# New priorities and new landing times for the planner of a fused attention and mixture-of-experts kernel

## Chip, cores and metric

The kernel runs on one core of one Trainium2 chip. The metric is device time in microseconds (us) of one execution. A core has four compute engines that the text names as the profile does: PE (TensorE, matmuls), DVE (VectorE), ACT (ScalarE) and POOL (GpSimd). SP (SyncE) mostly issues DMAs. Each engine takes its own instructions strictly in the order in which the program gave them to it.

## What is computed

Sliding-window attention with four sink tokens, and behind it a mixture of eight experts, of which each token takes the best two:

```python
scores = scale * np.matmul(q, k.transpose(0, 1, 3, 2))      # q, k, v: 4 x 8 x 768 x 64
keep = is_sink | in_window                                  # 4 sinks, window 128
scores = np.where(keep, scores, -1000000000.0)
scores = scores - np.max(scores, axis=-1, keepdims=True)
a = np.exp(scores)
a = a / (np.sum(a, axis=-1, keepdims=True) + 1e-09)
x = np.matmul(a, v)                                         # to 3072 tokens x 512
...
logits = x @ w_gate
noise_scale = np.log1p(np.exp(x @ w_noise))
noisy_logits = logits + noise_scale * noise
top2 = np.argpartition(-noisy_logits, 2, axis=1)[:, :2]     # weights: softmax over the two
...
h = np.maximum(x[mask] @ w1[e], 0.0)                        # 512 -> 1024, per expert
out[mask] += top2_w[mask, k, None] * (h @ w2[e])            # 1024 -> 512
```

## The kernel before

**Staging.** Part one (`phase_one`) is attention, the routing of the first three batches, and what the first expert needs. Part two (`phase_two`) is the routing of the last batch and the eight experts. Attention goes over 16 head pairs `g`, each in three tiles `n` of 2 x 128 queries, 48 tiles in all. Each tile is a chain over all engines. PE computes scores into a PSUM bank `S` (`qk`, L401). ACT copies the block before the diagonal (`prev`, L405) and DVE the diagonal block under its mask (`cur`, L410 and L412) into `cbuf`. DVE takes the row maximum (`mins`, L422), POOL subtracts it (`sub`, the helper of line 305), ACT takes the exponential (`exps`, L429), and DVE sums it for two tiles at once (`sums`, L432). PE turns the result (`ptr`, L464), ACT copies it to `CT` (`ptr_c`, L467), and DVE or POOL mask it to `CM` (`ptr_m`). The sinks go a way of their own: ACT copies them (`pcopy`, L451), PE turns them (L459), ACT copies them to `ps` (`sink_c`, L493) and PE multiplies (`sinks`, L502). PE multiplies with the values `vn` (L486) and with the difference of neighbouring value blocks `dv` (L489; the difference itself is line 305 on DVE or POOL). ACT copies the sum to `turned` (`pv_c`, L511), PE turns it back (`rows`, L516), DVE or ACT scale it (`rows_c`, L525), and SP stores it to `x_rows` in memory (L532).

Beside it run the logits of a batch (L710 to L726), its routing (L789 and on: the two best experts, a rank within each expert from a mask `m` by matmuls at L824, lists of tokens, L856 to L882), the gathers of the first expert's rows (`sg`, `xg`, issued by POOL), and the turning of these rows for PE (`rows_turn`, PE at L1093, ACT at L1102, DVE at line 305).

**Weights.** All weights are split into a rounded part and a remainder. For each chunk of 512 KB, `w_chunk` lets SP load it to a buffer `st` (L1129), ACT round it into `wr` or `w2a` (`hi`, L1138), and DVE or POOL take the remainder (`lo`). Five chunks of the first expert are loaded in part one. The same two `st` buffers hold the sinks' values, which ACT rounds to `vr` (L357). The first expert's matmuls are L1066 to L1068 (up) and L1337 to L1339 (down); a ReLU on ACT (L1318) and its remainder on DVE (L1326) lie between.

**What sets the order.** No order is written by hand. Every step is recorded by `Plan.op` with its engine, an assumed duration and a priority. `Plan.run` then plans: the engine that is free first takes, of its steps whose inputs are there by its reckoning, the one with the lowest number. The steps are emitted by planned start, and this is the order of each engine's queue. A transfer is planned as an SP step and a "DMA" step of assumed length `us`, and is taken to land a little later: 1.2 us, 0.6 more for a long one, plus `late`.

```python
    def dma(self, prio, fn, us, r=(), w=(), u=(), n=1, late=0):
        ...
        self.op("SP", .48 * n, prio, fn, r, list(w) + [("dma", d)], u, lat=.65)
        self.op("DMA", us, prio, None, list(r) + [("dma", d)], w, u, lat=1.2 + (.6 if us > .7 else 0) + late)
```

In attention a step's priority is its tile number plus a fraction plus `P(g, name)`: the table `PR` has one number for each kind of step, with an extra for the first two and last two head pairs, and the table `BY` has one more for each kind and each of the 16 pairs. Other steps of part one have numbers in `PR`: `ga` gathers, `gt` turning of gathered rows, `lg` logits, `rt` routing of the first three batches, `w1` the first expert's weights. Part two has its own table `P2`; its plan starts from the state in which the plan of part one ends. At run time the engines wait for semaphores, whatever the plan assumed.

Of the kernel before, what the change touches and what calls it, by code (L numbers as in the profile page):

```python
# [30 lines left out]
BY = dict(cur=(0, -1.82, -0.09, -4.77, 35.24, 11.33, 2.04, -10.64, 0.52, 0, -1.01, -3.26, 14.21, 1.62, 0.09, -1.4),
          cur1=(0.93, -1.05, -2.09, 0, -2.58, -1.8, -0.49, -4.53, 1.67, 0.36, -1.49, 1.77, 5.16, 0, 49.28, -0.04),
          mins=(6.57, 0.21, 57.07, 0.23, 0, -0.65, -13.4, 4.24, 13.09, -2.13, 0, -0.06, -0.69, 2.29, 67.31, 0.72),
          sub=(-1.09, 44.64, -1.41, -0.42, 4.26, 1.23, -3.67, -0.5, -0.79, 1.56, 235.35, 0.77, -1.93, -0.06, 2.36, 0),
          exps=(-7.52, 7.26, 2.07, 0.74, 0.15, -1.72, -0.45, -37.83, 0.43, 53.75, 1.62, -265.24, 1.55, -22.19, -1.22,
          2.06), sums=(0.42, -1.37, 9.97, 6.54, 0, 1.48, 1.11, 4.08, -5.15, -0.49, 0, 15.68, -4.9, -0.05, 7.41, 0),
          sums_i=(-0.24, 4.03, 0, -2.92, -0.07, -47.94, -0.24, 0.08, -0.02, 267.66, 10.52, 3.51, -12.76, 1.73, -1.63,
          0.51), pcopy=(-133.07, -3.49, 0.13, 0.44, -5.06, 2.59, -0.29, -3.31, 1.66, -3.27, -1.06, 2.44, -3.33, -1.68,
          231.11, -0.12), plow=(0, 0, 6.4, 0.11, 3.22, -9.99, 0, -0.73, 0, 0, 23.53, 0.11, -6.2, 1.96, 8.99, -409.97),
          ptr=(2.11, -1.38, -12.28, -2.62, 0.43, -21.26, -0.4, -5.17, 246.76, -0.54, -2.13, 38.22, -1.99, -1.89, 6.88,  # L40
          -1.57), ptr_c=(1.99, 16.57, -4.61, 1.02, -0.92, 0.3, 54.42, -6.52, 0, 0, 0, 35.55, -0.02, 0.04, -2.65,
          0.51), ptr_m=(41.67, 0, 2.33, -3.62, 18.7, -43.66, 0.3, -1.35, 0.78, -140.28, 5.45, 0, 1.7, 0.41, -2.24,
          -0.04), pv=(-36.95, 0.42, -8.83, -1.99, 8.78, -38.58, 2.7, 1.3, -57.52, -0.25, 3.87, 14.59, 0.81, 0.65,
          422.1, -0.97), sink_c=(-0.94, 5.09, 3.45, 11.6, 1.27, 4.39, -0.81, 2.55, -1.47, 2.51, 28.94, 0, -0.98, 0.1,
          0, 1.98), sinks=(-2.94, -5.28, 0.26, -0.7, 0.82, 0, 7.45, -0.38, 1.35, -0.62, 146.54, 2.21, 11.9, 0.31,
          -3.96, 2.78), pv_c=(15.49, 0, -2.23, -0.55, 1.03, 2.26, -0.17, -12.06, -0.32, 3.46, 339.15, 0, -3.91, 12.59,
          -1.6, 3.11), rows=(2.11, 74.27, -3.07, -2.66, 3.83, 0, -6.89, 0.11, -0.29, 0.14, 6.26, 0.43, 0, -0.24,
          -0.69, 6.02), rows_c=(-0.79, 0.84, -0.51, 0, -1.43, 9.38, -0.78, 0, -0.36, -0.22, 3.48, 0, 0, 0.12, 0.46,
          5.39), qk=(0.36, 0.1, 0, -6.57, 0.71, 17.87, -230.29, 6.22, 2.06, 7.39, 0.12, 161.15, -6.58, 2.53, -1.41,
# [1756 lines left out]
```

## Time and profile before

| | us |
|---|---|
| median of 3 runs | 747.22 |
| lowest and highest | 745.27, 747.65 |
| profiled execution, its own time | 745.87 |
| span of that execution, first to last instruction | 744.2 |
| PE busy in it | 704.3 (95%) |
| DVE, ACT, POOL busy | 548.4, 409.9, 314.4 |

The page gives busy times for the whole span, which mixes stages of different kinds. The table by stage is read for each stage by itself: an engine's busy time against the length of the stage, and the granted clock of TensorE beside it (1.00 is 2.4 GHz, 0.50 is 1.2 GHz). Its columns are the busy times of PE, PEld (weight loads), DVE, ACT and POOL, in this order. The timeline has in brackets how long an engine was idle before an instruction and what ended that. Matmuls are pipelined, so that the times of single ones overlap.

### The profile page before, as it was taken

The page shows a single profiled execution, that of the slowest core. Times are in us where ns is not written, and L with a number is a line of the kernel's source. Part 1 is how long each engine was busy: PE and PEld are TensorE (multiplying, and loading weights), DVE is VectorE, ACT ScalarE, POOL GpSimd, SP SyncE. Part 2 cuts the span into 40 slices and gives each one's busy share as a digit, 9 for nine tenths or more (in the row PEclk, how much of TensorE's full clock was granted, in tenths as well). Part 3 has the DMA queues.
Part 4 walks back from the last instruction along what each step waited for, and adds up shares of the span by engine and source line. Part 5 has one row for each costly group of instructions (what it writes and reads, how often), then busy time and mean ns, then how long its engine had stood idle before and what let it go on. Part 6 is the DMA issues. An engine that isn't in the chain of part 4 may idle for free.

```text
span 744.2 us, 13428 instructions
## 1 busy us (share of the span) xinstructions
PE 704.3 (95%) x4731; PEld 588.0 (79%) x4731; DVE 548.4 (74%) x1282; ACT 409.9 (55%) x924; POOL 314.4 (42%) x431
## 2 busy tenths in 40 slices
PE   6999698898999999999999999999999999999995
PEld 3666465666677888988988998899899889889983
DVE  6888879996762688687879588766968878785620
ACT  4878669685421455465556466455655546554430
POOL 5667668678322643235205223431632440090022
PEclk9999799999999999999999999999999999999998
DMA  8565666736466999639645754866486292254233
GB/s 299 177 217 169 197 195 176 228 108 159 121 176 200 231 321 279 184 110 198 221 136 117 216 177 103 180 176 191 113 218 199 81 251 61 90 108 91 58 44 44
DMA packets 87319, 123.13 MB, mean 165 GB/s; under 512 B 18640, under 2 KB 55376, under 8 KB 87248
## 3 DMA queue, kind: packets, MB, share of 16 engines
q1 hardware_dynamic: 75856, 94.64, 40.5%
q0 software_dynamic: 11392, 27.60, 19.0%
q8 instruction: 38, 0.62, 0.4%
q14 instruction: 33, 0.27, 0.1%
HBM read 81.49 MB, written 40.73 MB: 164 GB/s over the span
## 4 chain that ended last, share of the span: by engine, by line
PE 71%; DVE 12%; DMA 7%; ACT 4%; POOL 3%; issue 2%; SPq 0%; POOLq 0%; ACTq 0%; DVEq 0%
PE Y L1473 28%; PE B L1442 9%; PE B L1443 9%; PE B L1444 9%; DMA xg<-x_sorted 4%; PE S L401 3%; PE B L486 2%; PE B L464 2%; PE B L489 2%; PE Y L1476 1%; DMA sg<-x_rows,idg 1%; DVE x L305 1%; DMA st<-in_w1c 1%; DVE mn L422 1%; PE B L1067 1%
## 5 line engine op out<-in xcount | busy, mean ns | idle before, releaser
L1361 POOL DMA_INDIRECT out<-tmp,idx x34 | 80.3, 2362 | 168.6 <-ACT tmp L1346 164.1
L1443 PE MATMUL B<-x,wr 128*128 128x384 f32 (+1 forms) x392 | 134.9, 344 | 1.4 <-DVE x L305 1.4
L1473 PE MATMUL Y<-w2a,hb 128*128 128x512 f32 x504 | 129.2, 395 | 0.0
L1473 PE MATMUL Y<-w2b,hb 128*128 128x512 f32 x504 | 125.4, 392 | 0.7 <-DVE hb L1466 0.7
L1473 PEld LDWEIGHTS Y<-w2b,hb 128*128 128x128 f32 x504 | 94.4, 188 | 21.1 <-DVE hb L1466 1.1
L1473 PEld LDWEIGHTS Y<-w2a,hb 128*128 128x128 f32 x504 | 94.3, 188 | 19.2
L1443 PEld LDWEIGHTS B<-x,wr 128*128 128x128 f32 x392 | 73.6, 188 | 4.8 <-DVE x L305 2.1
L1444 PE MATMUL B<-xe,wr 128*128 128x384 f32 (+1 forms) x224 | 76.8, 343 | 0.0
L1442 PE MATMUL B<-xe,wr 128*128 128x384 f32 (+1 forms) x224 | 76.8, 343 | 0.0
L305 DVE TENSOR_TENSOR wr<-st,wr 128x512 fp32r<-128x512 f32 (+1 forms) x86 | 59.4, 696 | 12.7 <-ACT wr L1179 12.3
L305 POOL TENSOR_TENSOR cbuf<-cbuf,mn 128x528 f32<-128x528 f32 x48 | 53.9, 1125 | 21.5 <-DVE mn L422 14.6
L1442 PE MATMUL B<-x,wr 128*128 128x384 f32 (+1 forms) x168 | 58.1, 346 | 1.2 <-DVE tmp L1460 0.7
L1444 PE MATMUL B<-x,wr 128*128 128x384 f32 (+1 forms) x168 | 57.6, 343 | 0.0
L401 PE MATMUL S<-kq 64*64 64x196 f32 (+1 forms) x768 | 50.7, 366 | 5.9 <-DVE cbuf L412 2.7
L1179 ACT ACTIVATE wr<-st 128x512 fp32r<-128x512 f32 x84 | 52.0, 624 | 6.7 <-DVE st L305 6.3
L1030 POOL COPY spacer<-hb 1x1 f32<-1x1 f32 x38 | 12.1, 319 | 91.4 <-ACT hb L1463 88.7
L1457 ACT ACTIVATE tmp<-B 128x384 f32<-128x384 f32 (+1 forms) x56 | 28.0, 500 | 40.5 <-PE B L1444 36.5
L1361 POOL DMA_INDIRECT out<-turned,idx x18 | 31.8, 1766 | 39.8 <-ACT turned L1346 36.5
L1346 ACT ACTIVATE tmp<-Y,wc 128x512 f32<-128x512 f32 x31 | 21.3, 687 | 46.6 <-PE Y L1473 35.7
L1442 PEld LDWEIGHTS B<-xe,wr 128*128 128x128 f32 x224 | 42.1, 188 | 2.1
L1015 POOL DMA_INDIRECT sg<-x_rows,rt_idi x30 | 31.1, 1036 | 27.2 <-DMA x_sorted<-sg 12.6
L1444 PEld LDWEIGHTS B<-xe,wr 128*128 128x128 f32 x224 | 42.0, 188 | 0.2
(311 smaller groups left out, 1605.8 us busy)
## 6 DMA issues: line engine op xcount, KB each, us to landing
st<-in_w1c SPq DMA_DIRECT2D x32, 512.0 KB, 4.6
st<-in_w2c SPq DMA_DIRECT2D x32, 512.0 KB, 4.6
kq<-in_qk_t SPq DMA_DIRECT2D x15, 780.0 KB, 5.0
xg<-x_sorted SPq DMA_DIRECT2D x42, 272.0 KB, 4.1
x_sorted<-sg SPq DMA_DIRECT2D x30, 272.0 KB, 2.9
out<-zt SPq DMA_DIRECT2D x31, 256.0 KB, 4.3
vn<-in_v SPq DMA_DIRECT2D x16, 384.0 KB, 4.1
x_rows<-strip SPq DMA_DIRECT2D x48, 128.0 KB, 2.6
```

What stands on the lines that cost most here:

```text
L305: eng.tensor_tensor(out, a, b, op=OP.subtract)
L401: nc.tensor.matmul(whole[x, h, c0:c1], kq(g)[r, KS + 128 * j + 64 * s:KS + 128 * j + 64 * s + 64], kq(g)[r, o + c0:o + c1], start=True, st ...
L464: nc.tensor.transpose(p[:, u, :], C(n)[:, u, :128], idf)
L1015: nc.gpsimd.indirect_dma_start(out=stage(), out_offset=None, in_=xbuf, in_offset=bass.IndirectOffsetOnAxis(ap=cst["idw"]()[:, sh.TE * e + ...
L1179: plan.op("ACT", .03 + .255 * m, z, lambda: nc.scalar.activation(h(), src(), AF.Copy), r=[st], w=[(*key, b)] + old, u=[key, ex], lat=P2["s ...
L1346: nc.scalar.activation(get("y", Y[e, t], [128, DM]), get("Y", Y[e, t]), AF.Copy, scale=c["wc"][e % 2][:, t:t + 1])
L1361: d = nc.gpsimd.indirect_dma_start(out=out, out_offset=bass.IndirectOffsetOnAxis(ap=c["idx"][:size(e, t), e, t:t + 1], axis=0), in_=get("y ...
L1442: nc.tensor.matmul(p, wh, h, start=start and not k, stop=False, skip_group_check=True)
L1443: nc.tensor.matmul(p, wh, l, start=False, stop=False, skip_group_check=True)
L1444: nc.tensor.matmul(p, wl, h, start=False, stop=k == 1, skip_group_check=True)
L1457: nc.scalar.activation(u_of(e, k), src(), AF.Copy)
L1473: nc.tensor.matmul(p, h[:, x * (CAP + R) + 128 * t:x * (CAP + R) + 128 * t + 128], w[:, y], start=(f == 0 and x + y == 0), stop=(f == FC - ...
```

## The change

Two tables get new numbers, and some transfers are taken by the planner to land later. Nothing else is different: the same instructions with the same shapes run on the same engines. In the changed kernel a line below 60 is three further down than before. Of `PR`, six entries: `ga` 49.85 to 49.66, `gt` 3.95 to −21.71, `lg` 4.53 to −352.25, `rt` 0.34 to −120.41, `w1` 0 to −1.74, and a new `ll` = 4.05 for the last batch's logits, which had 0.5 by default. Of `BY`, all rows. The core of the diff, with one row of the table for its kind:

```diff
-          exps_9=0.19, ga=49.85, gt=3.95, lg=4.53, load_qk=-1.69, load_v=-1.08, mins=-2.22, mins_0=-5.85,
+          exps_9=0.19, ga=49.66, gt=-21.71, lg=-352.25, load_qk=-1.69, load_v=-1.08, mins=-2.22, mins_0=-5.85,
...
-BY = dict(cur=(0, -1.82, -0.09, -4.77, 35.24, 11.33, 2.04, -10.64, 0.52, 0, -1.01, -3.26, 14.21, 1.62, 0.09, -1.4),
+BY = dict(cur=(3.57, -13.88, 0.28, 0.46, 40.3, 11.34, -114.12, -161.0, -17.8, -22.04, 14.14, -3.47, -7.68, -85.27,
+          7.71, -45.51), cur1=(-33.65, 7.81, -38.13, -7.15, -33.59, -26.72, 5.35, 0.04, 2.2, 10.64, 1.58, -236.46,
...
-        plan.dma(n + .7, lambda n=n: rows_d(n), .37, r=[("xr", n)], w=[("xrow", n)])
+        plan.dma(n + .7, lambda n=n: rows_d(n), .37, r=[("xr", n)], w=[("xrow", n)], late=.8)
...
-        plan.dma(z, lambda: load_kq(g, gi), 2.3 if gi is None else .95, n=1 if gi is None else 2, w=[("kq", g, i) for i in (range(NJ) if gi is None else (gi,))],
+        plan.dma(z, lambda: load_kq(g, gi), 2.3 if gi is None else .95, n=1 if gi is None else 2, late=2.0 if gi is None else .5, w=[("kq", g, i) for i in (range(NJ) if gi is None else (gi,))],
...
-        plan.dma((g - 1) * NJ + PR.get("load_v", 1) + BY.get("load_v", ZERO)[g], lambda: load_v(g), 1.15, w=[("vn", g)])
+        plan.dma((g - 1) * NJ + PR.get("load_v", 1) + BY.get("load_v", ZERO)[g], lambda: load_v(g), 1.15, w=[("vn", g)], late=2.5)
...
-            plan.dma((z if g else -1996.5) + BY.get("load_st", ZERO)[g], lambda b=b: sink_values(b), 1.35, w=[("st", vst[b])])
+            plan.dma((z if g else -1996.5) + BY.get("load_st", ZERO)[g], lambda b=b: sink_values(b), 1.35, w=[("st", vst[b])], late=3)
...
-    plan.dma(z, load, 1.35, r=list(first) + ([("at", e)] if e else []), w=[("st", n)], late=P2["late"] if e else 0)
+    plan.dma(z, load, 1.35, r=list(first) + ([("at", e)] if e else []), w=[("st", n)], late=P2["late"] if e else 3.5)
```

What this does to the order is seen at three places: the first load of expert weights (on SP and on ACT), the routing of the third batch, and that of the last.

On SP, around the first load of expert weights (`st<-in_w1c`; `kq` and `vn` are loads of attention, `x_rows` its stores, `out<-zt` writes zeros). Before:

```order
L379 DMA vn<-in_v 128x768
L532 DMA x_rows<-strip 128x2x128
L373 DMA kq<-in_qk_t 128x1560
L1629 DMA out<-zt 128x512
L1129 DMA st<-in_w1c 128x1024
L373 DMA kq<-in_qk_t 128x1560
```

Now:

```order
L376 DMA kq<-in_qk_t 128x1560
L1632 DMA out<-zt 128x512
L1132 DMA st<-in_w1c 128x1024
L535 DMA x_rows<-strip 128x2x128
L1632 DMA out<-zt 128x512
L535 DMA x_rows<-strip 128x2x128
L382 DMA vn<-in_v 128x768
L535 DMA x_rows<-strip 128x2x128
L1632 DMA out<-zt 128x512
L376 DMA kq<-in_qk_t 128x1560
```

A load of `kq` stood directly behind the weights; the next one is now seven rows behind.

On ACT, the rounding of that load (`wr<-st`) with what stands ahead of it. Before:

```order
L405 ACTIVATE cbuf<-S_81 128x2x132
L451 ACTIVATE pcbuf<-cbuf 128x16x4
L405 ACTIVATE cbuf<-S_82 128x2x132
L429 ACTIVATE cbuf<-cbuf 128x4x132 x2
L451 ACTIVATE pcbuf<-cbuf 128x16x4
L1138 ACTIVATE wr<-st 128x1024
L429 ACTIVATE cbuf<-cbuf 128x4x132
L511 ACTIVATE turned<-B_77 128x256
```

Now:

```order
L470 ACTIVATE CT<-B_74 128x512
L496 ACTIVATE ps<-B_76 128x128
L717 ACTIVATE lt<-B_75 128x256
L408 ACTIVATE cbuf<-S_82 128x2x132
L432 ACTIVATE cbuf<-cbuf 128x4x132
L408 ACTIVATE cbuf<-S_81 128x2x132
L360 ACTIVATE vr<-st 128x1024
L1141 ACTIVATE wr<-st 128x1024
L514 ACTIVATE turned<-B_76 128x256
```

Counted in the order in which the program emits, six ACT instructions (the six ahead of it above) lay between the load's issue and its rounding; now it is 16, of which the last seven are shown.

On DVE, the end of the third batch's routing (`rt_tc` are its last tables) and what follows. Before:

```order
L882 TENSOR_TENSOR rt_tc_2753<-io_92,rt_tv 128x336
L432 TENSOR_REDUCE sm<-cbuf 128x8
L443 RECIPROCAL ri<-sm 128x4x2
L525 TENSOR_TENSOR strip<-B_75,ri 128x256
L910 SCALAR_TENSOR_TENSOR idg<-B_77,ga 128x4
```

Now:

```order
L885 TENSOR_TENSOR rt_tc_2682<-io_92,rt_tv 128x336
L425 TENSOR_REDUCE mn<-cbuf 128x4
L415 COPY_PREDICATED cbuf<-le,S_82 128x2x128
L415 COPY_PREDICATED cbuf<-le,S_81 128x2x128
L425 TENSOR_REDUCE mn<-cbuf 128x4
L308 TENSOR_TENSOR dv<-vn 128x640
L913 SCALAR_TENSOR_TENSOR idg<-B_77,ga 128x4
```

The last row maxima of attention (L422 before) stood ahead of this routing; three of them, and three or four score copies (L412 before), now stand behind it.

On DVE, the routing of the last batch at the start of the experts, from its first logits step to the mask `m` that the rank matmuls read (`hb` is a ReLU remainder of the first expert). Before:

```order
L793 TENSOR_SCALAR turned<-turned 128x48
L1326 SCALAR_TENSOR_TENSOR hb<-B_76,hb 128x512
L305 TENSOR_TENSOR turned<-turned 128x48
L1326 SCALAR_TENSOR_TENSOR hb<-B_74,hb 128x512
L796 TENSOR_TENSOR turned<-turned 128x48
L797 TENSOR_TENSOR turned<-turned 128x48
L798 TENSOR_TENSOR turned<-turned,nz 128x48
L799 TENSOR_TENSOR turned<-lg,turned 128x48
L803 MAX turned<-turned 128x8 x6
```

Now:

```order
L796 TENSOR_SCALAR turned<-turned 128x48
L308 TENSOR_TENSOR turned<-turned 128x48
L799 TENSOR_TENSOR turned<-turned 128x48
L800 TENSOR_TENSOR turned<-turned 128x48
L801 TENSOR_TENSOR turned<-turned,nz 128x48
L802 TENSOR_TENSOR turned<-lg,turned 128x48
L1329 SCALAR_TENSOR_TENSOR hb<-B_76,hb 128x512
L806 MAX turned<-turned 128x8 x6
```

Two remainders stood between these steps, one is left, and it has moved behind the noise steps. On PE the rank matmul (L824) stood behind 48 expert matmuls and now stands behind 30.

## Rows read from the trace of the kernel before

**Rows 1.** The page's parts 1 and 2: busy times, granted clock by slice

```profile
PE 704.3 (95%) x4731; PEld 588.0 (79%) x4731; DVE 548.4 (74%) x1282; ACT 409.9 (55%) x924; POOL 314.4 (42%) x431
...
PEclk9999799999999999999999999999999999999998
```

**Rows 2.** Table by stage: length, busy time (count) by engine, clock, DMA share, GB/s

```profile
20.00:80.00 60.00, 56.32 (x770) 39.18 (x766) 52.98 (x124) 50.53 (x160) 41.73 (x71) 1.00 0.59 182
80.00:96.00 16.00, 10.35 (x100) 6.87 (x99) 11.70 (x25) 8.80 (x21) 11.32 (x14) 0.68 0.63 212
96.00:125.00 29.00, 26.86 (x370) 18.88 (x371) 26.09 (x71) 23.90 (x70) 21.50 (x36) 1.00 0.66 201
125.00:137.00 12.00, 10.46 (x134) 7.03 (x129) 11.48 (x25) 7.61 (x24) 9.23 (x15) 0.86 0.72 188
137.00:170.00 33.00, 31.35 (x418) 21.59 (x418) 30.86 (x79) 27.68 (x83) 24.67 (x44) 1.00 0.52 162
170.00:193.70 23.70, 19.27 (x209) 13.54 (x205) 14.81 (x37) 11.57 (x31) 13.05 (x21) 1.00 0.61 157
```

**Rows 3.** The same table, cut where the granted clock is low

```profile
84.66:94.90 10.24, 6.66 (x56) 4.86 (x52) 6.26 (x12) 5.05 (x13) 6.91 (x7) 0.50 0.60 223
...
132.45:135.86 3.41, 3.41 (x40) 2.03 (x37) 2.93 (x6) 1.66 (x5) 1.71 (x2) 0.50 0.65 198
```

**Rows 4.** Chain of waits, 80 to 92 us: start, us, what

```profile
82.34 8.82 DMA st<-in_w1c
```

**Rows 5.** Issues of line 1129 before 200 us: time to landing

```profile
DMA to landing us min/median/max: 4.2/5.6/8.8
```

**Rows 6.** Timeline of ACT, 84 to 97 us: start, us, what, [idle <-releaser]

```profile
87.83 0.26 ACT L451 ACTIVATE pcbuf<-cbuf 128x64 fp32r<-128x64 f32 x1
91.18 1.06 ACT L1138 ACTIVATE wr<-st 128x1024 fp32r<-128x1024 f32 x1 [3.10 <-DMA st<-in_w1c]
```

**Rows 7.** Timeline of PE, 81 to 137 us

```profile
85.69 1.36 PE L401 MATMUL S<-kq 64*64 64x128 f32 x16 [0.98 <-DVE cbuf L412]
...
90.55 0.69 PE L489 MATMUL B<-CM,dv 128*64 128x128 f32 x4 [2.45 <-DVE dv L305]
...
125.27 0.78 PE L401 MATMUL S<-kq 64*64 64x128 f32 x16
...
131.07 0.44 PE L502 MATMUL B<-ps,vr 64*128 64x128 f32 x4 [1.13 <-ACT ps L493]
```

**Rows 8.** Timeline of DVE, 86 to 101 us

```profile
89.73 0.77 DVE L305 TENSOR_TENSOR dv<-vn 128x640 f32<-128x640 f32 x1
93.88 0.42 DVE L525 TENSOR_TENSOR strip<-B,ri 128x256 f32<-128x256 f32 x1 [3.38 <-ACT turned L511]
```

**Rows 9.** Table by stage again, inside the stage 80 to 96

```profile
84.00:88.00 4.00, 3.02 (x40) 1.63 (x32) 4.00 (x9) 2.81 (x7) 2.37 (x4) 0.58 1.01 366
```

**Rows 10.** PE's waits from 193.7 us on: waited for, us, times, longest

```profile
PE B L1093 <- DMA sg<-x_rows,idg: 1.4, 2, 1.2
PE B L1443 <- DVE x L305: 1.4, 2, 1.1
```

**Rows 11.** Timeline of PE, 191 to 207 us

```profile
193.74 0.50 PE L1066 MATMUL B<-xe,wr 128*128 128x512 f32 x1 [0.74 <-ACT xe L1102]
...
205.49 0.20 PE L824 MATMUL B<-m,tri 128*128 128x48 bf16 x1
```

**Rows 12.** Timeline of DVE, 193 to 206 us

```profile
200.80 0.69 DVE L1326 SCALAR_TENSOR_TENSOR hb<-B,hb 128x512 fp32r<-128x512 f32 x1 [1.92 <-ACT hb L1318]
...
204.08 0.21 DVE L816 TENSOR_TENSOR m<-oh 128x48 bf16<-128x48 f32 x1
```

**Rows 13.** Timeline of DVE, 165 to 180 us

```profile
169.13 0.69 DVE L422 TENSOR_REDUCE mn<-cbuf 128x4 f32<-128x528 f32 x1
169.75 0.14 DVE L856 TENSOR_TENSOR vm<-slot,B 128x4 f32<-128x4 f32 x1
...
173.13 1.12 DVE L882 TENSOR_TENSOR rt_tc<-io,rt_tv 128x336 f16<-128x336 f16 x2
```

More of the change, by code (lines that the diff above doesn't have):

```diff
@@ L27 @@
           pv_c_9=-1.08, qk=-14.69, qk_0=-0.57, qk_9=-10.67, rows=1.38, rows_0=0.53, rows_9=-53.32, rows_c=3.24,
-          rows_c_0=-0.84, rows_c_9=-1.82, rt=0.34, sink_c=-0.22, sink_c_0=-0.01, sink_c_9=2.24, sinks=1.43,
+          rows_c_0=-0.84, rows_c_9=-1.82, rt=-120.41, sink_c=-0.22, sink_c_0=-0.01, sink_c_9=2.24, sinks=1.43,
           sinks_0=10.1, sinks_9=3.8, sub=0.04, sub_0=-3.77, sub_9=0.87, sums=0.22, sums_0=2.8, sums_i=-11.64,
-          sums_i_9=-13.22, w1=0, pct=-0.28)
-BY = dict(cur=(0, -1.82, -0.09, -4.77, 35.24, 11.33, 2.04, -10.64, 0.52, 0, -1.01, -3.26, 14.21, 1.62, 0.09, -1.4),
[L32 to L49, printed above, removed]
-          -19.77), prev=(0.07, 0.42, -2.2, -0.97, -6.51, -0.17, 1.55, -0.75, 1.64, -0.4, 0, -0.03, 0.98, -2.35, 0.19,
-          -15.25), nosink=(2.49, 0, -2.37, 0.05, -0.25, 0.25, 10.01, 0.28, -0.51, 30.86, 1.18, -12.06, -0.4, 2.54,
-          1.57, 16.51), dv=(-1.94, -239.87, -15.26, 0, 3.2, -0.16, 29.29, -0.59, -1.52, 194.71, 4.73, 5.74, -112.07,
-          0.05, 0.08, -23.12), pct=(0, -8.69, -0.46, 0.01, 20.61, 6.07, -4.03, -48.64, 5.06, -7.63, 1.03, 0, -0.47, 0,
-          32.35, -0.34), load_qk=(0, 0, -0.61, 0, 0.52, 3.45, 4.11, 11.45, 2.66, -2.48, -1.53, 9.96, -0.92, 0.21, 0,
-          1.93), load_v=(0, -0.41, 0.74, 3.68, 5.68, -86.67, -0.06, -0.06, -0.26, -25.59, 22.86, 0.94, -15.02, -5.4,
-          1.25, 0.32), load_st=(-5.35, 0, 0, 0, 6.23, 0, 0, 0, -6.07, 0, 0, 0, -5.64, 0, 0, 0), sink_v=(-1.98, 0, 0,
-          0, -1.15, 0, 0, 0, -8.24, 0, 0, 0, 23.03, 0, 0, 0))
@@ L583, in attention @@
         else:
-            plan.dma(-1997, lambda: load_v(0), 1.15, w=[("vn", 0)])
+            plan.dma(-1997, lambda: load_v(0), 1.15, w=[("vn", 0)], late=1)
         if g % HP == 0:
             b, z = g // HP, (g - HP) * NJ if g else -6
-            plan.dma((z if g else -1996.5) + BY.get("load_st", ZERO)[g], lambda b=b: sink_values(b), 1.35, w=[("st", vst[b])])
+            plan.dma((z if g else -1996.5) + BY.get("load_st", ZERO)[g], lambda b=b: sink_values(b), 1.35, w=[("st", vst[b])], late=3)
             z += 9 if g else 0
```

29 lines of the change are left out of this document (added).

## The prediction

> **What bounds the kernel now.** I read the page's busy shares first, then the table by stage, then what PE waits for in the stages that stand out. PE is busy for 704.3 of 744.2 us and TensorE's granted clock is full almost everywhere [rows 1], so the time can fall in two ways: PE stands still less, or it runs less at the low clock. The table by stage shows where either is to be had [rows 2]. From 20 to 80 us PE is busy for 56.32 of 60 us, a share of 0.939. From 80 to 96 it is busy for 10.35 of 16 with a mean granted clock of 0.68, and from 125 to 137 for 10.46 of 12 at 0.86. The last attention tiles (170 to 193.7) give 19.27 of 23.7. From 193.7 on, PE is nearly full. A change that only reorders part one has its prize in the hole of 80 to 96.
>
> What makes the hole is read backward. The chain of waits has one piece of 8.82 us in it: the first load of expert weights, issued at 82.34 [rows 4]. ACT finishes a small copy at about 88.09 (87.83 + 0.26), and its next instruction, the rounding of that load, starts at 91.18 with 3.10 us of waiting for the DMA in front of it [rows 6]. ACT works in order, so the softmax's exponentials and the copies behind it wait too. DVE, done with `dv` at 90.50, stands 3.38 us for one of these copies [rows 8]. PE had already waited 0.98 us for `cur` and then 2.45 us for `dv` [rows 7]. The second wait is not ACT's: DVE had work without a break then, 4.00 us in the four from 84 to 88 [rows 9]. Over these gaps the granted clock is down: it is 0.50, that is 1.2 GHz, for 10.24 us in which PE is busy for 6.66 [rows 3], and the sixteen 128-wide score matmuls take 1.36 us where they take 0.78 at the full clock [rows 7]. The low stretch of 3.41 us from 132.45 follows a wait of 1.13 us for `ps` at 131.07 [rows 3, 7].
>
> **The change, part by part.** No duration, shape or count of instructions changes; only the order of part one does, and that part two starts from a different end state.
>
> *Later landings.* They move rounding steps away from loads. The first load shows it in the order: six ACT instructions were emitted between load and rounding, now 16. ACT runs 160 instructions in the 60 us of the steady stage [rows 2], one per 0.375 us, so 16 of them are at least 6.0 us. In the hole the six took 5.75 us (82.34 to 88.09), 0.96 each, by which 16 are 15.3 us. The loads of line 1129 land in 4.2 to 8.8 us, median 5.6 [rows 5]. So a median landing is covered at either pace, and the slowest is short by at most 2.8 us at the faster pace: ACT's wait goes from 3.10 to between 0 and 2.8, and I take 0. What covers it is the work of the next tiles on ACT, and if that is gone the price is the old one. The next whole `kq` also stands seven rows behind the load on SP, not directly behind it, so the load has less beside it: from 84 to 88 us the DMA engines were full (1.01) at 366 GB/s [rows 9]. The Trainium skill ("DMA: Bandwidth & Descriptors", "Anatomy of one DMA — SWDGE (gpsimd) path") gives a transfer about 2.0 us plus its bytes at 436 GB/s, as an estimate 3.2 us for these 512 KB, by which no landing would need the longer lead and the sum would lose its largest term. The trace disagrees: its shortest landing here is 4.2 us, and these loads share the engines with others.
>
> *What the hole is worth.* Its bounds come from the two engines with most work in it. By DVE: 11.70 us of work at the steady stage's share of 52.98/60 = 0.883 takes 13.25 us, a gain of 2.75. By PE: the 6.66 us at half clock are 3.33 at full, so the work is 10.35 − 3.33 = 7.02, which at 0.939 takes 7.5 us, a gain of 8.5. The middle is 5.6. A second count takes 20 to 170 us together, since work left over in one tile falls to the next: DVE has 52.98 + 11.70 + 26.09 + 11.48 + 30.86 = 133.1 us of work there, PE 56.32 + 7.02 + 26.86 + (10.46 − 1.70) + 31.35 = 130.3 at full clock [rows 2, 3]. DVE is the fuller of the two. At its share of the stage 96 to 125 (0.900) it needs 147.9 us, at that of 137 to 170 (0.935) 142.4: gains of 2.1 and 7.6 against the 150, the middle share giving 4.9. This count has the low clock of 132 us in it. Between 5.6 and 4.9 **I take −5.2 us, with ends −2.1 and −8.5**.
>
> *Routing of the first three batches and logits first.* `rt` and `lg` go far down, so that a batch's routing on DVE runs ahead of attention as soon as it is ready. The third batch's chain, from 169.75 to 174.25, started when the last maximum of attention had just begun (169.13) [rows 13], with none left behind it; now three maxima and score copies stand behind it. That takes DVE from PE for up to 4.5 us if PE has nothing queued, and gives the same 4.5 us back in the tail, where PE is idle for 23.70 − 19.27 = 4.4 us [rows 2]. Bounds +4.5 and −4.4; I take 0, as work is only moved between neighbours.
>
> *The first expert and the last routing.* In before, the first expert matmul starts at 193.74 and the last batch's rank at 205.49, after 48 expert matmuls, 0.245 us each [rows 11]. Now 30 stand ahead of it: 18 × 0.245 = 4.4 us earlier. The mask `m` it reads was ready at 204.29, 10.55 us after the first expert matmul [rows 12]. In DVE's order the second ReLU remainder stood ahead of the last logits steps, with 1.92 us of waiting and 0.69 of work [rows 12]; now only one remainder stands ahead of the mask. So `m` can be 2.6 us earlier, at 7.9 us, against a rank that PE reaches at 30 × 0.245 = 7.35: a wait of 0.6. Gathers then start some 4.4 − 0.6 = 3.8 us earlier, which would take away the 1.4 us of PE's waits for the gather of `sg` and part of the 1.4 us for `x` [rows 10]. Bounds: −2.8 with no new wait, and +3.2 (10.55 − 7.35) if `m` is as late as before; I take −0.7, nearer to the first since the order shows the second remainder gone.
>
> *The rest.* Later landings of `kq`, `vn` and `vsink` put their users later, and none of the waits named above is for one of these, so 0. Sum: −5.2 − 0.7 = −5.9 us, the profiled execution's 745.87 becoming 740.0. The median is 1.35 above the profiled execution, so **the forecast is 741.3 us**.
>
> **The rivals.**
> *DVE keeps the pace.* The wait on ACT goes, but the tiles behind it are held by DVE, which had no idle time from 84 to 88 us [rows 9]. Then the gain is 2.1 to 2.75 us with nothing in part two: 744.5 to 745.1. For it: the second count, and PE's 2.45 us wait that was DVE's. Against it: DVE's own 3.38 us of standing came from ACT.
>
> *The 8.82 us were an accident.* A load that lands in its 4.2 us minimum [rows 5] is there at 86.5, before ACT asks at 88.09: with no wait there in the usual run, the new landing times are worth nothing and the time is 747.2. Against it: the profiled execution with the wait is not slower than the median. This is also the result by the figure of the Trainium skill ("DMA: Bandwidth & Descriptors", "Anatomy of one DMA — SWDGE (gpsimd) path") above, and the trace speaks against that figure for these loads.
>
> *Routing first costs PE.* Three routings run ahead of attention now. If two of them stop PE for 4.5 us each and the clock falls once as it did in the hole (6.66 / 2 = 3.3 us), the cost is 12.3 against a gain of 5.9: 747.2 − 5.9 + 12.3 = 753.6. It decides from waits behind routing of 5.9 us in all (no gain), 8.2 (slower by over 0.3%). Against it: maxima and score copies still stand between the routing's rows, and PE has three tiles under way.
>
> *More than the hole.* Tiles pack at DVE's best share (−7.6), the waits of part two go (−2.8) and half of the tail's 4.4 us is filled (−2.2): 747.2 − 12.6 = 734.6.
>
> **How the numbers follow.** Forecast (737.5 to 744.4) 0.50, DVE keeps the pace 0.16, accident 0.10, routing costs PE 0.12, more than the hole 0.12. The predicted time is that of the first. The range 735.5 to 747.5 takes in the first three and half of the last, and leaves out 0.12 + 0.06 = 0.18. A measurement of this kernel can tell about 0.3% (2.2 us) from no change: below 745.0 is faster, above 749.5 slower. Faster: 0.50 + 0.12 + 0.09 of the second case = 0.71. Same: 0.07 of the second and 0.08 of the third = 0.15. Slower: 0.12 and 0.02 of the third = 0.14.
>
> **What would show it.** In the profile after, the first rounding of expert weights on ACT starts with no DMA in front of it; the table by stage has no slice below 0.9 clock between 80 and 140 us; the first expert matmul starts at 187.5 to 189.5 us, not 193.74; and the rank follows it by about 8 us. If the clock is full and that matmul still starts after 191, DVE keeps the pace. If PE waits over 3 us for `cur` or for a maximum behind a routing chain, the slower rival is right. A gather wait of over 2 us after 200 us would make the term of part two wrong. A low stretch at a new place would undo the first term.

## The result, and the profile after

The changed kernel takes 730.17 us (median of 4 runs, 728.37 to 731.16), the kernel before in the same comparison 747.43 (4 runs, 745.27 to 748.66). The ratio is 0.9769, with a 95% interval of 0.974 to 0.9799: 17.3 us faster. The forecast was 741.3 with a range of 735.5 to 747.5, so the direction was right and the size came out nearly three times as large, beyond the largest rival (734.6) too.

The page of the changed kernel, busy time by engine (share of the span, count) and granted clock by slice of 18.2 us, which answers [rows 1]:

```profile
PE 700.2 (96%) x4731; PEld 587.9 (81%) x4731; DVE 549.5 (75%) x1282; ACT 410.5 (56%) x924; POOL 312.7 (43%) x431
...
PEclk9999999999999999999999999999999999999998
```

The work is the same (DVE 548.4 before, 549.5 now). The dip of the clock row in its fifth slice (74 to 93 us) is gone; the last slice is as before. The table by stage, cut as in [rows 2] (length, busy time with count of PE, PEld, DVE, ACT and POOL, granted clock, DMA share, GB/s):

```profile
20.00:80.00 60.00, 57.69 (x778) 40.89 (x778) 55.66 (x130) 52.08 (x162) 43.96 (x75) 1.00 0.66 193
80.00:96.00 16.00, 15.86 (x214) 10.36 (x210) 15.19 (x33) 12.45 (x31) 10.63 (x14) 1.00 0.86 292
96.00:125.00 29.00, 25.76 (x325) 17.66 (x323) 27.20 (x69) 23.03 (x72) 23.95 (x41) 0.94 0.56 165
125.00:137.00 12.00, 11.95 (x164) 8.64 (x160) 11.77 (x25) 10.37 (x28) 8.61 (x15) 1.00 0.99 340
137.00:170.00 33.00, 30.66 (x406) 21.89 (x400) 31.77 (x85) 26.77 (x82) 28.19 (x51) 1.00 0.43 117
170.00:193.70 23.70, 21.45 (x163) 15.79 (x162) 15.61 (x57) 8.64 (x18) 9.25 (x11) 0.93 0.49 148
```

From 80 to 96 us PE is busy for 15.86 of 16 us, where it was 10.35, 6.66 of them at the low clock [rows 3]. The last row is not the same work as before: the experts begin inside it. On PE's timeline (start, us, what, idle before and its releaser) the first expert matmul and the last batch's rank:

```profile
180.37 0.50 PE L1069 MATMUL B<-xe,wr 128*128 128x512 f32 x1 [0.74 <-ACT xe L1105]
...
189.49 0.20 PE L827 MATMUL B<-m,tri 128*128 128x48 bf16 x1
```

So the experts start 13.37 us earlier (193.74 before, [rows 11]), and from there to the end of the span it takes 728.1 − 180.37 = 547.73 us against 744.2 − 193.74 = 550.46. The span's gain of 16.1 us is 13.4 in part one and 2.7 in part two.

Where part one's 13.4 us lie is counted from the two traces: in each stretch, the time in which PE did nothing, and its busy time times (1 − granted clock), which is what the low clock cost.

| Stretch, us | Before: idle, low clock | After: idle, low clock | Change |
|---|---|---|---|
| 0 to 20 | 6.4, 6.7 | 6.5, 5.3 | −1.3 |
| 20 to 80 | 3.7, 0 | 2.3, 0 | −1.4 |
| 80 to 100 | 5.7, 3.3 | 0.3, 0 | −8.7 |
| 100 to 140 | 3.7, 1.7 | 3.1, 1.7 | −0.6 |
| 140 to the first expert | 6.1, 0 | 4.3, 0 | −1.9 |
| work at full clock | 156.4 | 156.8 | +0.4 |

The first row needs care. The table by stage would show a clock of 1.00 from 0 to 20 us, but the trace has no clock reading before 19.81 us (before) and 17.18 us (after). The same products, eight matmuls each, show that the clock was low before 19.81 in the kernel before:

```profile
17.78 1.12 PE L486 MATMUL B<-CT,vn 128*64 128x128 f32 x8
...
20.36 0.66 PE L486 MATMUL B<-CT,vn 128*64 128x128 f32 x8
```

So PE's busy time ahead of the first reading is counted at 0.50. By this count three traces with the start of the kernel before (before, e9, e11) have 5.3 to 6.7 us in that place, and the −1.3 of the first row is not put down to the change.

Two thirds of the 13.4 us are the hole of 80 to 100 us. A low clock is still there, at new places (table by stage of after): from 110 to 118 us, behind a gap of PE of 1.31 us for a score copy at 103.95 and smaller ones, and at the start of the experts (181.03 to 184.44):

```profile
110.00:118.00 8.00, 7.10 (x78) 5.58 (x78) 7.77 (x19) 5.70 (x21) 5.70 (x12) 0.79 0.57 143
180.00:190.00 10.00, 9.30 (x50) 7.16 (x51) 5.84 (x34) 3.76 (x8) 1.80 (x4) 0.83 0.35 121
```

ACT's timeline of after, and the answer on the load's line 1132 before 200 us, stand against [rows 6] and [rows 5]:

```profile
90.02 1.04 ACT L1141 ACTIVATE wr<-st 128x1024 fp32r<-128x1024 f32 x1
```

```profile
DMA to landing us min/median/max: 3.7/5.5/8.0
```

The load was issued at 78.65 and is rounded 11.4 us later, with no wait in front.

### The profile page after: what moved, and what is told of

The parts are those of the page before. It is cut to its first block, busy times and chain, and to the rows that moved or that the text cites. A ratio compares the mean times of both kernels' runs of the same rounds, so it can differ in the third digit from the quotient of the medians.

```text
span 728.1 us, 13418 instructions
## 1 busy us (share of the span) xinstructions
PE 700.2 (96%) x4731; PEld 587.9 (81%) x4731; DVE 549.5 (75%) x1282; ACT 410.5 (56%) x924; POOL 312.7 (43%) x431
## 4 chain that ended last, share of the span: by engine, by line
PE 71%; DVE 14%; DMA 4%; ACT 3%; issue 3%; POOL 2%; SPq 0%; POOLq 0%; DVEq 0%; ACTq 0%
PE Y L1476 28%; PE B L1446 9%; PE B L1445 9%; PE B L1447 9%; DMA xg<-x_sorted 3%; PE S L404 2%; DVE cbuf L415 2%; DVE mn L425 2%; PE B L1070 1%; PE Y L1479 1%; PE B L1071 1%; PE B L1069 1%; DVE sm L435 1%; DVE x L308 1%; PE B L467 1%
## 5 line engine op out<-in xcount | busy, mean ns | idle before, releaser
L404 PE MATMUL S<-kq 64*64 64x196 f32 (+1 forms) x768 | 48.5, 355 | 4.6 <-DVE cbuf L415 2.5
L1018 POOL DMA_INDIRECT sg<-x_rows,rt_idi x30 | 31.7, 1057 | 29.8 <-DMA x_sorted<-sg 15.3
```

The lines of the kernel that those rows point to most:

```text
L404: nc.tensor.matmul(whole[x, h, c0:c1], kq(g)[r, KS + 128 * j + 64 * s:KS + 128 * j + 64 * s + 64], kq(g)[r, o + c0:o + c1], start=True, st ...
L1018: nc.gpsimd.indirect_dma_start(out=stage(), out_offset=None, in_=xbuf, in_offset=bass.IndirectOffsetOnAxis(ap=cst["idw"]()[:, sh.TE * e + ...
```

## The experiments

All kernels are compared with the kernel before, run beside them; it had medians of 746.9 to 748.9 us there. Moves in an order are written as the rows of the queue that change place.

### Is it ACT's wait for the load?

**e1** is the kernel before with the first rounding put nine rows later on ACT, the one wait that the prediction blamed:

```diff
 L451 ACTIVATE pcbuf<-cbuf 128x16x4
-L1138 ACTIVATE wr<-st 128x1024
 L429 ACTIVATE cbuf<-cbuf 128x4x132
...
 L467 ACTIVATE CT<-B_74 128x512
+L1138 ACTIVATE wr<-st 128x1024
 L405 ACTIVATE cbuf<-S_81 128x2x132
```

> The kernel before in its old order, with one thing moved: the rounding of the first weight load on ACT (and the remainder behind it on POOL) stands nine rows later in ACT's queue, some 15 instructions behind the load as in the changed kernel. Theory of TensorE's pace: ACT no longer stands for 3.10 us, the hole of 80 to 96 us closes at PE's pace, gaps and low clock both gone, about -8.7 us, 738 to 740 us. Rival, the prediction's DVE's pace: the tiles are held by DVE's work, -2 to -3 us, 744 to 746 us. Rival, an accident: the wait is not there in the usual run, 747 us.

Measured: 748.5 us, ratio 1.0016 (0.9987 to 1.0046). Nothing. The timeline of e1 (start, us, engine and what, idle before) says why:

```profile
90.13 0.69 DVE L422 TENSOR_REDUCE mn<-cbuf 128x4 f32<-128x528 f32 x1
...
91.68 0.70 PE L489 MATMUL B<-CM,dv 128*64 128x128 f32 x4 [2.46 <-DVE dv L305]
...
92.58 0.64 ACT L429 ACTIVATE cbuf<-cbuf 128x528 f32<-128x528 f32 x1 [3.37 <-POOL cbuf L305]
```

The exponential that stood behind the rounding does not start earlier. It now waits 3.37 us for POOL's subtraction, whose maximum DVE takes at 90.13, behind two sums. The wait for the load had covered this one. PE's 2.46 us for `dv` is the same as in [rows 7].

The trace of e11 (described further down; its only edit lies behind 180 us) is a second trace of the old order in the hole, and there the load landed earlier (7.1 us after its issue). ACT:

```profile
88.55 1.06 ACT L1138 ACTIVATE wr<-st 128x1024 fp32r<-128x1024 f32 x1 [0.92 <-DMA st<-in_w1c]
```

ACT waits 0.92 us and not 3.10, and the hole is as large: 4.9 us of standing and 3.7 of low clock from 80 to 100 us, against 5.7 and 3.3.

**e2** is the opposite, the changed kernel with the rounding one ACT instruction behind its load's issue:

```diff
 L470 ACTIVATE CT<-B_74 128x512
+L1141 ACTIVATE wr<-st 128x1024
 L496 ACTIVATE ps<-B_76 128x128
...
 L360 ACTIVATE vr<-st 128x1024
-L1141 ACTIVATE wr<-st 128x1024
 L514 ACTIVATE turned<-B_76 128x256
```

> The changed kernel with only that rounding moved the other way: it stands directly behind the next ACT instruction after the load's issue, so that ACT asks for it at about 81.3 us while the load, issued at 78.65, lands 3.7 to 6.1 us after that. Theory of TensorE's pace: ACT stands for 1 to 3.5 us, PE waits and the granted clock falls, +3 to +9 us, 733 to 739 us. Rival, DVE's pace: the tiles in flight cover it, +0 to +3 us, 730 to 733 us.

Measured: 737.5 us, ratio 0.9848 (0.9816 to 0.988), 5.9 us over the changed kernel by the ratios (0.0079 of 747.4). The timeline of e2, and its stage 80 to 96:

```profile
86.73 1.06 ACT L1141 ACTIVATE wr<-st 128x1024 fp32r<-128x1024 f32 x1 [5.44 <-DMA st<-in_w1c]
...
88.01 0.69 PE L505 MATMUL B<-ps,vr 64*128 64x128 f32 x4 [5.79 <-ACT ps L496]
```

```profile
80.00:96.00 16.00, 10.21 (x100) 7.13 (x100) 6.55 (x14) 6.09 (x15) 4.45 (x8) 0.68 0.49 175
```

The hole is back, as large as before (9.1 us by my count, 9.0 before). So a wait of ACT for this load can make such a hole, and some lead is needed; in the kernel before, though, taking the wait away buys nothing.

### Which late thing is it, then?

**e5** adds to e1 the other wait that PE showed: `dv` of that pair is put earlier on DVE. **e6** does that alone.

```diff
 L422 TENSOR_REDUCE mn<-cbuf 128x4 x2
+L305 TENSOR_TENSOR dv<-vn 128x640
 L432 TENSOR_REDUCE sm<-cbuf 128x8
...
 L443 RECIPROCAL ri<-sm 128x4x2
-L305 TENSOR_TENSOR dv<-vn 128x640
 L525 TENSOR_TENSOR strip<-B_77,ri 128x256
```

> The kernel before with two things moved in the queues: the rounding of the first weight load nine rows later on ACT (as in the run before that moved it alone and gained nothing), and the value difference dv of head pair 6 ahead of the sums that stood before it on DVE, at about 82 instead of 89.7 us. Theory of two covers: PE's 2.45 us for dv and ACT's 3.10 us for the load lay side by side, each hiding behind the other; with both gone the second half of the hole closes, -3 to -6 us, 741 to 744 us. Rival, DVE's work holds the tiles whatever stands first: within 2 us of the kernel before.

> The kernel before with only the difference dv of head pair 6 moved ahead on DVE. Theory of two covers: PE's wait for dv is gone, but the copies behind ACT's 3.10 us wait for the load are late next, 0 to -1.5 us, 745.5 to 747 us. Rival, the order on DVE alone made the hole: -3 to -6 us, 741 to 744 us.

Measured: e5 749.16 us, 1.0023 (0.9999 to 1.0048); e6 750.06, 1.0025 (0.999 to 1.0059). Nothing again: in e5 PE's wait for `dv` is gone and one for ACT's `turned`, behind the late exponential, stands in its place (PE of e5):

```profile
93.35 0.44 PE L516 MATMUL B<-idf,turned 128*128 128x128 f32 x2 [1.70 <-ACT turned L511]
```

**e9** takes the third one too: the late maximum of DVE stands ahead of the two sums, and its subtraction on POOL follows. **e10** is e9 without the move on ACT.

```diff
 L412 COPY_PREDICATED cbuf<-le,S_82 128x2x128
+L422 TENSOR_REDUCE mn<-cbuf 128x4
 L432 TENSOR_REDUCE sm<-cbuf 128x8
...
 L432 TENSOR_REDUCE sm<-cbuf 128x8
-L422 TENSOR_REDUCE mn<-cbuf 128x4
```

> The kernel before with a third thing moved beside the two of the earlier run: the rounding of the first load later on ACT, dv of pair 6 earlier on DVE, and the row maximum of tile 26 (with POOL's subtraction behind it) ahead of the two sums on DVE, since ACT had waited 3.08 us for that subtraction once the other two were out of the way. Theory of several covers: these three were the whole list, PE's gaps between 86 and 94 us go, and -3 to -6 us come back, 741 to 745 us. Rival, a backlog: DVE has too much to do there after the first routing, the next late thing takes over, within 2 us of the kernel before.

> The same without the move on ACT: dv and the maximum are early, and ACT's wait for the load is the only one left of the three. Theory of several covers: now the load's 3.10 us are seen on their own, and this run is 2 to 4 us slower than the one with all three moved. Rival, the backlog: both runs are alike within 2 us, and like the kernel before.

Measured: e9 746.07 us, 0.9957 (0.9926 to 0.9987); e10 746.04, 0.9974 (0.9945 to 1.0003). Some 2 to 3 us; e10's interval reaches no change, and the two cannot be told apart. PE of e9 from 82 to 89 us, and its stage:

```profile
84.19 0.28 PE L459 MATMUL B<-idr,pcbuf 128*128 128x128 f32 x1 [2.03 <-POOL pcbuf L305]
85.53 1.27 PE L401 MATMUL S<-kq 64*64 64x196 f32 x16 [1.07 <-DVE cbuf L412]
87.48 1.36 PE L401 MATMUL S<-kq 64*64 64x128 f32 x16 [0.68 <-DVE cbuf L412]
```

```profile
80.00:96.00 16.00, 11.92 (x140) 8.80 (x138) 14.27 (x27) 9.18 (x24) 9.95 (x16) 0.79 0.69 224
```

The gaps of 88 to 94 us are gone, those of 82 to 88 have stayed, and with them the low clock. In e10 the rounding stands at its old place on ACT and starts at 91.00, where the load lands (7.0 us after its issue), after 0.14 us of standing; so what that wait costs by itself once the others are gone was not measured.

**e13** goes at the earlier gaps with the theory that DVE fell behind in the first batch's routing, whose end starts at 71.9 us, so that later score copies came late: its rows are spread, one row of attention between two of them. **e14** is e13 and e9 together.

```diff
 L868 TENSOR_REDUCE r_122<-rt_ro 128x12
+L412 COPY_PREDICATED cbuf<-le,S_82 128x2x128
 L869 SCALAR_TENSOR_TENSOR rt_g<-rt_ix,r_122 128x12
+L412 COPY_PREDICATED cbuf<-le,S_81 128x2x128
 L873 TENSOR_SCALAR rt_vl<-r_122 128x12
```

> The kernel before with the end of the first batch's routing on DVE spread: between every two of its steps from line 868 on stands one more attention step, the row maxima and score copies that it held up come first, and the matmuls that read it stand six DVE instructions later on PE. Theory that this routing makes the hole: attention's chain to the sinks (maximum, subtraction, exponential, copy) is not late any more, PE's gaps of 1.45 to 2.04 us at 81 to 88 us go and the low clock with them, -4 to -8 us, 740 to 744 us. Rival, DVE's work is only moved: the gaps move some microseconds on, within 2 us of the kernel before.

> The same spreading with the three moves of the earlier run (rounding of the first load, dv of pair 6, maximum of tile 26) beside it. Theory that routing and the three waits are the whole hole: 80 to 96 us look like their neighbours, -6 to -9 us, 739 to 742 us. Rival, a backlog of DVE that no order of these steps removes: as the three moves alone, 744 to 747 us.

Measured: e13 751.77 us, 1.0055 (1.0026 to 1.0083); e14 747.95, 1.0007 (0.9979 to 1.0036). Worse, or nothing. PE of e13 has the gaps at other places:

```profile
82.98 1.93 PE L401 MATMUL S<-kq 64*64 64x196 f32 x16 [2.46 <-DVE cbuf L410]
...
94.47 0.69 PE L489 MATMUL B<-CM,dv 128*64 128x128 f32 x4 [2.53 <-DVE dv L305]
```

**e17** gives PE work for the gaps: value products of two tiles stand ahead of the score matmuls, their copies on ACT with them, beside e9's moves and a still earlier `dv`.

```diff
 L401 MATMUL S_82<-kq 64x196 x4
+L486 MATMUL B_77<-CT,vn 64x128 x4
+L489 MATMUL B_77<-CM,dv 64x128 x2
 L459 MATMUL B_76<-idr,pcbuf 128x128
+L486 MATMUL B_75<-CT,vn 64x128 x4
+L489 MATMUL B_75<-CM,dv 64x128 x4
 L401 MATMUL S_81<-kq 64x196 x4
```

> The kernel before with PE's own order changed at the hole, beside the three moves of an earlier run: the products with the values of tiles 18 and 19, whose inputs are there at 80 us but for dv of pair 6, stand ahead of the score matmuls that PE waited at, and dv of pair 6 stands on DVE at 78 us; the copies of their results on ACT follow. Theory that the hole is work that lay ready behind waiting instructions: PE is busy through 81 to 88 us, the granted clock does not fall, -6 to -9 us, 739 to 742 us. Rival, DVE's work is the limit there: PE only waits later, 744 to 747 us, as with the three moves alone.

Measured: 747.2 us, 0.9992 (0.9957 to 1.0028). Its stages, and PE at 90 us:

```profile
80.00:88.00 8.00, 5.55 (x90) 3.49 (x86) 7.80 (x17) 5.44 (x15) 5.89 (x9) 1.00 0.86 263
90.00:100.00 10.00, 9.11 (x75) 6.97 (x75) 4.49 (x11) 4.77 (x11) 3.69 (x7) 0.66 0.52 165
```

```profile
90.54 1.11 PE L464 MATMUL B<-idf,cbuf 128*128 128x128 f32 x4 [2.25 <-ACT CT L467]
```

The clock stays full to 88 us, though PE still stands for 2.45 of these 8 us; then PE waits 2.25 us for ACT's copy of `CT`, and the clock falls behind that. The gap has only moved. None of these moves, alone or together, closes the hole: by the count above, 6.7 to 12.5 us are left of 9.0 in the ten traces with such moves (e15 and e18, below, among them). Which part of the changed order closes it was not isolated; the next section narrows it.

### Landings or table?

**e3** is the changed kernel with the old tables, **e4** with the old landings:

```diff
-        plan.dma(n + .7, lambda n=n: rows_d(n), .37, r=[("xr", n)], w=[("xrow", n)], late=.8)
+        plan.dma(n + .7, lambda n=n: rows_d(n), .37, r=[("xr", n)], w=[("xrow", n)])
```

(one line of e4's for its kind). Three more are the changed kernel with one thing taken back: **e7** the landing of the first expert weights (3.5 to 0), **e8** that of the row stores (the diff just shown, alone), **e16** the two table entries that let routing run first:

```diff
-lg=-352.25
+lg=4.53
-rt=-120.41
+rt=0.34
```

> The new landing times with the old tables: one half of the change alone. If the landing times carry the gain: the first rounding has no DMA in front of it and the time is 735 to 740 us. Rival, the old numbers fit the old order only: other waits of 5 us and more appear, and the time is 747 us or over.

> The new tables with the old landing times: the other half alone. If the landing times carry the gain: a rounding on ACT waits for its load again by 2 us or more, and the time is 737 to 745 us. Rival, the tables carry it: 730 to 733 us. If both are needed, it is over 747 us.

> The changed kernel with one landing time taken back: that of the first expert's weights, 3.5 to 0. The whole order from there on is planned anew with the tables as they are. Theory that this landing time carries the gain: a rounding on ACT waits 2 us or more for its load, and the time is 736 to 742 us. Rival, the tables carry it: within 2 us of the changed kernel's 730.

> The changed kernel with another landing time taken back, that of the stores of finished rows, 0.8 to 0; no instruction of attention waits for such a store except through its buffer. Theory that the tables fit one plan only, and any shift of the plan costs: 735 to 742 us, with new waits at places that have nothing to do with the stores. Rival, landing times matter where they were wrong: within 2 us of 730.

> The changed kernel with two of its numbers taken back, the priorities of the middle batches' routing (-120.41 to 0.34) and logits (-352.25 to 4.53). Theory that the tables fit one plan: 738 to 755 us, losses spread over part one. Rival, that routing first is worth the shorter way to the first expert and no more: +2 to +4 us, 732 to 734 us, with the loss after 140 us.

| Kernel | Median, us | Ratio (95%) | Over the changed kernel, by ratio |
|---|---|---|---|
| e3, landings alone | 748.3 | 1.0028 (1.0 to 1.0055) | +19 |
| e4, tables alone | 742.5 | 0.9915 (0.9881 to 0.9948) | +11 |
| e7 | 741.73 | 0.9902 (0.9872 to 0.9932) | +10 |
| e8 | 754.25 | 1.0067 (1.0039 to 1.0095) | +22 |
| e16 | 744.6 | 0.9959 (0.9933 to 0.9984) | +14 |

Ratios are times 747.4 in the last column. Landings alone gain nothing, tables alone 6 us, both 17. Taking back any one of three parts loses 10 to 22 us, together more than the whole.

The hole is not where these kernels lose most. From 80 to 100 us PE stands for 1.2 us in e4, 1.4 in e7, 1.2 in e8 and 2.3 in e16, all at the full clock, and for 1.3 in e3 with 1.7 of low clock. The stage and ACT's rounding in e4, which has the new tables and every old landing time:

```profile
80.00:96.00 16.00, 14.79 (x195) 9.94 (x194) 14.13 (x30) 12.33 (x32) 12.71 (x19) 1.00 0.87 264
```

```profile
90.51 1.05 ACT L1141 ACTIVATE wr<-st 128x1024 fp32r<-128x1024 f32 x1
```

So the new tables close most of the hole without the later landings, and the new landings do so with the old tables (e3). The sign that the expectations of e4 and e7 named for the landing times, a rounding that waits 2 us or more for its load, did not come (no wait in e4, 0.45 us in e7); their times lie in that theory's range all the same, which is luck. In e3 no rounding waits for its load, as expected, and the gain did not come. The losses of the last three lie in the main behind 96 us, at other places in each, one row of each here: e16 at 96 to 125, e7 at 137 to 170, e8 at 125 to 137 (order of columns as above):

```profile
96.00:125.00 29.00, 24.46 (x258) 16.19 (x251) 23.17 (x63) 18.76 (x58) 19.05 (x34) 0.77 0.56 173
```

```profile
137.00:170.00 33.00, 29.10 (x351) 20.65 (x349) 27.95 (x77) 23.19 (x73) 22.88 (x48) 0.84 0.37 115
```

```profile
125.00:137.00 12.00, 8.16 (x100) 4.76 (x98) 11.88 (x23) 7.75 (x24) 9.95 (x13) 0.81 0.57 155
```

So the gain cannot be shared out to the parts. The table's numbers are good for one set of landings; each of these edits made the planner choose a new order, with gaps and low clocks of its own.

### A wait that the prediction had not seen

In the kernel before, DVE copies four columns of gate weights (`wc`) that come with the first expert's gathers. They stand between the last attention work, and DVE waits for each gather. **e11** puts them last on DVE's queue of part one; **e12** does the same to the changed kernel; **e15** is e14 with it, **e18** e17 with it.

```diff
-L1265 COPY wc_148<-sg 128x1
 L474 TENSOR_TENSOR CM<-B_74,ge 128x512
-L1265 COPY wc_148<-sg 128x1
 L525 TENSOR_TENSOR strip<-B_75,ri 128x256
...
 L305 TENSOR_TENSOR xe<-B_77,xe 128x4x128
+L1265 COPY wc_148<-sg 128x1 x2
```

> The kernel before with the four small copies of gate weights out of gathered rows (line 1265) put behind everything else of part one on DVE, so that DVE does not stand for a gather ahead of attention's last rows and logits. Theory that the tail hangs on this: PE's waits after 184 us (0.6 us in the profile of before, 2.8 in those of two runs above) go, and so does a low clock there, -1 to -4 us, 743 to 746 us. Rival, the tail hangs on the gathers and the turning of their rows, which stay where they are: within 1 us of the kernel before.

> The changed kernel with the same four copies put last on DVE. In its profile DVE waits 1.6 and 0.9 us for gathers there, but no wait of PE over 0.2 us follows from it. Theory that PE has its cover there: within 1 us of the changed kernel's 730. Rival: the rows and logits behind these copies come earlier, and with them the first expert, -1 to -2 us, 728 to 729 us.

> All moves by hand together: the spreading, the three moves, and the copies of gate weights last on DVE, which alone gave 4 to 5 us. Theory that these are separate places: the sum of their gains, 734 to 739 us. Rival, what comes early at one place waits at the next: no more than the best of them alone, 742 to 744 us.

> The same, with the four copies of gate weights last on DVE, which alone gave some 5 us. Theory of separate places, hole and tail: the sum, 734 to 738 us. Rival, what the hole gives back is waited for in the tail, where the gathers set the end: 741 to 744 us.

Measured: e11 743.1 us, 0.9938 (0.9909 to 0.9968); e12 729.02, 0.9736 (0.9708 to 0.9764); e15 743.22, 0.9948 (0.9914 to 0.9983); e18 743.03, 0.9939 (0.9907 to 0.9971). DVE of the kernel before, of e11, and of the changed kernel:

```profile
184.41 0.15 DVE L1265 COPY wc<-sg 128x1 f32<-128x1 f32 x1 [0.87 <-DMA sg<-x_rows,idg]
187.29 0.15 DVE L1265 COPY wc<-xg 128x1 f32<-128x1 f32 x1 [2.27 <-DMA xg<-x_rows,idg]
```

```profile
193.48 0.21 DVE L1265 COPY wc<-sg 128x1 f32<-128x1 f32 x2
```

```profile
174.49 0.15 DVE L1268 COPY wc<-sg 128x1 f32<-128x1 f32 x1 [1.58 <-DMA sg<-x_rows,idg]
```

The waits, three of 3.9 us together before, are gone in e11, which is worth 4.6 us by the ratio (2.4 to 6.8); the other moves add nothing to it (e15, e18). Of the profiled runs, e11's shows 1.0 us of it before the first expert and 1.9 behind it. The changed kernel still waits there, 2.4 us, and e12 cannot be told from it: the intervals overlap (0.9708 to 0.9764, 0.974 to 0.9799).

## Why the prediction was right or wrong

**The cause of the hole failed.** The step read the wait that ended last on ACT, 3.10 us for the load, as the origin of the hole. In e1 that wait is gone, the hole is as large (8.9 us by the count above, 9.0 before) and the time is the same. The order of time had said so: the clock fell at 84.66 [rows 3], ACT's wait began at 88.09, and PE's four gaps in the hole (1.45, 0.42, 0.98 and 2.45 of 5.7 us) ended by 90.55, before the rounding started at 91.18. The first, the one that the prediction does not have:

```profile
83.03 0.28 PE L459 MATMUL B<-idr,pcbuf 128*128 128x128 f32 x1 [1.45 <-POOL pcbuf L305]
```

Beside the load stood a subtraction, a maximum, `dv` and score copies, late on other engines. `dv` was in the prediction's own rows, as a wait that was not ACT's; the subtraction and the maximum were seen only when the load's wait was taken away. And e4 closes most of the hole with the old landing times, so that the later landings, which the prediction held for the cause of its largest term, are not needed for it. The rival that held the 8.82 us landing for an accident was right that the wait is worth nothing in the kernel before, and wrong in the time that it drew from that: the new order did not only remove the wait.

**The lead was right.** 16 ACT instructions were to take 6.0 to 15.3 us and cover the load; they took 11.4 and the rounding waits for nothing. e2 shows that some cover is needed; 7.8 us are enough in e7.

**The size of the hole failed, at its bounds.** The step went to the middle between DVE's bound (2.75) and PE's (8.5). It came out at PE's: 8.7 us from 80 to 100. What misled was DVE's share. DVE's 0.883 of the steady stage was taken as what DVE can do, but DVE was not the limit in that stage; it was as busy as the order let it be. In the changed kernel it works 55.66 of 60 us (0.928) in that stage, 15.19 of 16 (0.949) in the hole's, and from 20 to 170 us 55.66 + 15.19 + 27.20 + 11.77 + 31.77 = 141.6 of 150, a share of 0.944, above the best share (0.935) that I had allowed.

**The second count had the right answer in it and I set it aside.** It gave PE 130.3 us of work at the full clock from 20 to 170. At PE's share of the steady stage (0.939) that takes 138.8, a gain of 11.2 against the 150. The changed kernel does 140.2 us of such work in these 150, at which pace 130.3 take 139.4: a gain of 10.6. I went on with DVE, "the fuller", by 2.8 us of 133. Part one's term was −5.2; −13.4 was measured, of which −1.3 at the start is not put down to the change. No rival had all of it: "more than the hole" stopped at DVE's share too (−7.6), and added half of the tail (−2.2; the last stretch gave −1.9).

**Routing first, taken at 0,** cannot be confirmed as a term by itself. The third batch's step `rt_g` is at 156.09 where it was at 170.37, and the first gather at 168.04 where it was at 178.93; e16 loses 14 us. But e16 loses it from 96 us on, spread, with a whole other order. The fear that routing stops PE was wrong for the third batch: from 120 to 181 us PE waits for score copies behind DVE's work 0.6 us in all.

**Part two, −0.7, came out as −2.7,** close to the end that I had given as −2.8. The rank follows the first expert matmul by 9.12 us (forecast about 8, before 11.75). It did not wait for `m`, which was ready at 8.3 us:

```profile
188.46 0.21 DVE L819 TENSOR_TENSOR m<-oh 128x48 bf16<-128x48 f32 x1
```

What delayed it is the low clock of 181.03 to 184.44, in which the expert matmuls take 0.63 us each and behind it 0.40. In e12, whose order is the same on PE, that stretch ran at the full clock: the first expert matmul is at 178.93 and the rank 7.60 us behind it, near the 7.35 of the prediction's count, with no wait for `m`:

```profile
186.53 0.20 PE L827 MATMUL B<-m,tri 128*128 128x48 bf16 x1
```

The two waits for `sg` [rows 10] are gone. PE's first transpose of these gathers comes at the same distance as before (25.8 us), but at 24.4 in e12, without the low clock at the start. The runs side by side, profiled spans:

| Kernel | Rank behind first expert, us | First expert to end, us |
|---|---|---|
| after, e2, e3, e12, e16 | 7.6 to 9.1 | 547.5 to 547.9 |
| before and the other fourteen | 11.7 to 13.5 | 546.6 to 551.9 |

With an early rank part two is short in all five traces; with a late one it can be as short. So the −2.7 cannot be put down to the rank alone, and that it came close to the −2.8 is in part luck. What decides in the second row was not tested.

**The things to look for:** no DMA wait at the first rounding, held. No slice below 0.9 clock from 80 to 140, held in the table as cut above, but the finer one has 0.79 from 110 to 118; this low stretch at a new place did not undo the first term, though the prediction had said that it would. First expert at 187.5 to 189.5 us, wrong (180.37). Rank about 8 us behind it, nearly. No wait for a gather over 2 us on PE, held: the longest PE wait behind 180 us is

```profile
PE B L1446 <- DVE x L308: 1.0, 1, 1.0
```

## What to carry to other kernels

A wait on the path is worth only the time to the next late thing, and it explains no gap that ends before it does: before you price its removal, list for each engine what would release the same instruction second, and the next one behind it. Bound the gain of a reordering by the work of the engine that carries the kernel, at its full clock; the share at which a helper engine runs is no limit unless rows show that it was never without work there. Where a planner's table sets the order, its numbers and the durations that it assumes are one thing: take a part back and you measure another order, not that part.
